# Two gate tiles, wide copies and other homes for batch 0's sums in a fused attention and gated-convolution kernel

## The chip, the cores and the metric

The kernel runs on one core of a Trainium2 chip. The core has five engines, each with its own instruction stream that is worked off in order: TensorE (PE in the profile; its weight loads are PEld), VectorE (DVE), ScalarE (ACT), GpSimd (POOL) and SyncE (SP), which here only issues loads. An engine that reaches an instruction whose inputs are not there stands still, with all that is queued behind it. TensorE writes into PSUM, eight banks of 128 partitions x 512 fp32 values; GpSimd has no part in PSUM here, so whatever TensorE produces is read by VectorE or ScalarE. The metric is the device time of one execution in microseconds (us); lower is better.

## The reference

`x` is [4, 12800, 128] (four batches of 12800 rows), `inducing` is [32, 128]; all outputs are fp32.

```python
def mab(q, kv):                                   # softmax attention
    s = scale * (q @ kv.transpose(0, 2, 1))       # scale = 1/sqrt(128)
    s = s - s.max(-1, keepdims=True)
    a = np.exp(s)
    a /= a.sum(-1, keepdims=True) + 1e-09
    return a @ kv
h = mab(I, x)            # stage 1: 32 queries over all 12800 rows -> h [32, 128] per batch
y = mab(x, h)            # stage 2: each row of x over the 32 rows of h
gate = 1 / (1 + np.exp(-conv(y)))                 # causal depthwise convolution with 5 taps along the rows
out = (gate * (y @ w_val)) @ w_out
```

Stage 2 of a batch cannot begin before its `h` is complete, and `h` needs every row of the batch.

## The kernel before, in words

Each batch is cut into seven units of 2048 rows (one of them 512; "w = 512" and "w = 128" in the code, per group of four). A unit of stage 1 loads `x` transposed (tile `xT`, 1 MB), forms the scores with four matmuls (`a_mm`, tile `s`), takes their maximum and transposes them on VectorE (`a_max`, `a_tr`, tile `e`). When all seven maxima of the batch are there, the batch's maximum `mb` is made (`p_ml` to `p_mc`); then each unit subtracts it (`a_sub`), takes exp on ScalarE (`a_exp`), adds to the sums (`a_z`) and multiplies with `x` in row layout (`a_h`, tile `h`, reading tile `xk`). `p_z`, `p_h` and `p_hq` finish `h`, and `p_v` to `p_we` fold `h`, the taps and `w_val` into small stationary weights `wstk`.

A unit of stage 2 has the scores of its rows (`b_mm`), a softmax over 32 values spread over VectorE, GpSimd and ScalarE (`b_tr` to `b_norm`), the way back to a matmul operand in two fp16 halves (`b_back`, `b_hi`, `b_lo`, tile `hl`), then the gate (`c_gate`, 60 matmuls on four 32-row strips, 4 PSUM banks, tile `g`), two tanh (`c_tanh`), the value product (`c_val`, 12 matmuls, tile `v` in the same four banks, so it starts when both tanh have read the gate), gate times value on VectorE (`c_gv`, two halves, tile `gt`), four output matmuls (`c_out`, tile `o`, two banks in turn) and their copies (`c_ev`, tile `os`), after which the unit is stored.

For batches 1 to 3 the row layout `xk` is loaded (`load_k`). For batch 0 it is made on the chip (`MADE(b)`): TensorE transposes four 128x128 blocks of `xT` into one bank of the four-bank tile `gp` (`a_kt`), and a 512-wide copy carries the bank to `xk` (`a_ke`). The four banks are one tile to the layer that places the waits. Batch 0's made tiles live in `xk` buffers for four units and in `xT` buffers for three (`TAGK`), so that only nine of the twelve `xT` buffers take loads at first.

The order of every engine's instructions is fixed when the program is built. `stage1` and `stage2` add tasks with an engine, a cost in us, a key and dependences; `Plan.order` is a list scheduler that picks the task that can start first, among those within `SLACK` of it the one with the lowest key. `KA` to `KS` and `OUTK` set the keys (`OUTK` says how late the output matmuls come), `BUFS` the number of buffers by tag.

Of the kernel before, what the change touches and what calls it, by code (L numbers as in the profile page):

```python
# [18 lines left out]
P = 128  # L19
M = 32  # L20
# [17 lines left out]
BUFS = dict(xT=12, xk=4, e=7, q=3, m=2, z=2, p=2, hl=3, gt=4, os=2, nm=2, wst=2, wst2=2, gsc=2, hq=2, s=1, x=1, o=2, g=1, gp=4)  # L38
# [3 lines left out]
SLACK = 0.14  # L42
OUTK = 1.21
KA, KB, KH, KC, KP, KS = -4.5, 0.69, 0.0, 0.5, 3.59, 1.94
# [3 lines left out]
def TAGK(b, u):  # L48
    return "xk" if 1 <= u <= BUFS["xk"] else "xT"

# [95 lines left out]
def tile_kernel(ctx: ExitStack, tc: tile.TileContext, xT, xk, inducing, w_val, conv_w, w_out, out):  # L146
# [89 lines left out]
    def load_k(b, u):  # L236
        t0, w = units(b)[u]
        n = w // M
        x = st[b, u, "xk"] = sbt("xk", [P, 16, P])
        nc.sync.dma_start(x[:, :n, :], xk[b, :, t0 // P:t0 // P + n, :])  # L240


    def a_kt(b, u, j):
        w = units(b)[u][1]
        if "gp" not in c_:
            c_["gp"], c_["gpn"] = ps("gp", "g", [P, G, 512]), 0
        k = st[b, u, j, "gp"] = c_["gpn"] % G
        c_["gpn"] += 1
        x = st[b, u, "xT"][:, :G * w].rearrange("p (t i) -> p i t", t=P)
        for i in range(4):  # L250
            T.transpose(c_["gp"][:, k, P * i:P * i + P], x[:, 4 * j + i], c_["identf"])  # L251

    def a_kx(b, u):
        st[b, u, "xk"] = sbt("xk", [P, 16, P], tag=TAGK(b, u))

    def a_ke(b, u, j, eng):
        k = st[b, u, j, "gp"]
        o = st[b, u, "xk"][:, 4 * j:4 * j + 4, :].rearrange("p i c -> p (i c)")
        if eng == "ACT":
            S.copy(o, c_["gp"][:, k, :])  # L260
        else:
            V.tensor_copy(o, c_["gp"][:, k, :])
# [43 lines left out]
    def a_sub(b, u):  # L306
        n = units(b)[u][1] // M
        e = st[b, u, "e"]
        Gp.tensor_tensor(e[:, :n], e[:, :n], bat[b]["mb"].broadcast_to([P, n, M]), ALU.subtract)  # L309
# [7 lines left out]
    def a_z(b, u, v):  # L317
# [3 lines left out]
        if "za" not in d:  # L321
            d["za"] = sbt("za", [P, 16, M])
        if MADE(b):
            V.tensor_reduce(d["za"][:, v, :], e[:, :n].rearrange("p i j -> p j i"), AX.X, ALU.add)  # L324
        elif v == 0:
# [4 lines left out]
    def a_h(b, u, v):  # L330
# [4 lines left out]
        e, x = st[b, u, "e"], st[b, u, "xk"]  # L335
        for i in range(n):
            s = i % G
            T.matmul(d["h"][M * s:M * s + M, :P], e[:, i, :], x[:, i, :],  # L338
# [3 lines left out]
    def p_z(b):  # L342
        d = bat[b]
        zl = d["zl"] = sbt("zl", [P, M])
        n = NU if MADE(b) else 16
        V.tensor_reduce(zl, d["za"][:, :n].rearrange("p i j -> p j i"), AX.X, ALU.add)
# [150 lines left out]
    def strips(b, u, bank, d, k, first, last):  # L497
        w = units(b)[u][1]
        h, wst = st[b, u, "hl"], bat[b]["wst"]
        for i, (part, wp) in enumerate(((0, 0), (0, 1), (1, 0))):  # L500
            for g in range(G):
                s = slice(M * g, M * g + M)
                T.matmul(bank[:, g, :w], wst[s, wp, k, :], h[s, part, 4 - d:4 - d + w],  # L503
                         start=first and i == 0, stop=last and i == 2, tile_position=(M * g, 0))

    def c_gate(b, u):
        bank = st[b, u, "g"] = ps("g", "g", [P, G, 512])
# [3 lines left out]
    def c_tanh(b, u, i):  # L511
        w = units(b)[u][1]
        t = st[b, u, i, "t"] = sbt("gt", [P, 2, 512])
        S.activation(t[:, :, :w], st[b, u, "g"][:, 2 * i:2 * i + 2, :w], AF.Tanh, scale=bat[b]["gsc"])  # L514

    def c_val(b, u):
        bank = st[b, u, "v"] = ps("v", "g", [P, G, 512])
        strips(b, u, bank, 0, TAPS, True, True)

    def c_gv(b, u, i):  # L520
        w = units(b)[u][1]
        t = st[b, u, i, "t"]
        V.scalar_tensor_tensor(t[:, :, :w], t[:, :, :w], 1.0, st[b, u, "v"][:, 2 * i:2 * i + 2, :w], ALU.add, ALU.mult)  # L523
# [37 lines left out]
    def stage1(b):  # L561
# [3 lines left out]
        made = [st[c, u, "kl"][0] for c in range(b) if MADE(c) for u in range(NU)]  # L565
        order = [(v + 1) % NU if b == 0 else v for v in range(NU)]
        kxs = {}
        if MADE(b):
            for u in order:
                kxs[u] = add("NONE", 0.0, -2000, a_kx, (b, u), alloc=TAGK(b, u))  # L570
            made = list(kxs.values())
        for v, u in enumerate(order):
            w = units(b)[u][1]
            key = KEY1(b, v)
            lt = st[b, u, "lt"] = last = add("SP", l(w, 0.1, 2.55), b * NU + v, load_t, (b, u), deps=[last] + made, alloc="xT", lat=2.0)
# [5 lines left out]
            xk, kx = [], kxs.get(u)  # L581
            if MADE(b):
                for j in range(w // P):
                    kt = add("PE", 0.46, -92.9 + 0.01 * v, a_kt, (b, u, j), deps=[lt] + xk[:1], uses=[lt], alloc="gp")
                    eng = "DVE" if v >= NU - 2 and j % 2 else "ACT"
                    xk.append(add(eng, 0.6, -92.9 + 0.01 * v, a_ke, (b, u, j, eng), deps=[kx], uses=[kt, kx]))
                gps.extend(xk)
            st[b, u, "kl"] = [kx] + xk
        if not MADE(b):
            for v, u in enumerate(order):  # L590
                w = units(b)[u][1]
                lk = last = add("SP", l(w, 0.1, 2.55), b * NU + v, load_k, (b, u), deps=[last], alloc="xk", lat=2.0)
                st[b, u, "kl"] = [lk]
# [7 lines left out]
        for v, u in enumerate(order):  # L601
# [3 lines left out]
            su = add("POOL", l(w, 0.3, 1.1), key, a_sub, (b, u), deps=[mc], uses=[tr])  # L605
            ex = add("ACT", l(w, 0.25, 0.64), key, a_exp, (b, u), deps=[su], uses=[tr])
            if MADE(b):
                z = add("DVE", l(w, 0.25, 0.68), key, a_z, (b, u, v), deps=[ex], uses=[tr])
                zs.append(z)
            else:  # L610
                z = add("POOL", l(w, 0.3, 1.1), key + 0.5, a_z, (b, u, v), deps=[ex] + ([z] if z else []), uses=[tr])
                zs = [z]
            lk = st[b, u, "kl"]
            if v == 0:
                h0 = h = add("PE", l(w, 0.25, 1.0), key, a_h, (b, u, v), deps=ph[b - 1:b] + [ex] + lk, uses=[tr] + lk[:1], alloc="x")
            else:
                h = add("PE", l(w, 0.25, 1.0), key, a_h, (b, u, v), deps=[ex, h] + lk, uses=[tr, h0] + lk[:1])
        k = KEYP(b)
        z = add("DVE", 0.35 if MADE(b) else 0.68, k, p_z, (b,), deps=zs)
# [16 lines left out]
    def stage2(b):  # L636
        nonlocal outs
        for u in range(NU):
# [17 lines left out]
            va = add("PE", l(w, 0.19, 0.76), key - 0.3, c_val, (b, u), deps=th, uses=[hi], alloc="g")  # L656
# [61 lines left out]
```

## Time and profile before

| what | value |
|---|---|
| time, median of 3 | 356.49 us (355.5 to 357.47) |
| profiled execution | 354.77 us, of which the span from first to last instruction is 352.9 us |
| PE busy | 313.2 us (89% of the span), mean granted clock 0.968 |
| DVE, ACT, POOL busy | 210.8, 171.1, 156.3 us |
| HBM traffic | 72.4 MB, 205 GB/s over the span |
| chain that ended last | PE 73%, ACT 9%, DVE 8%, POOL 5% of the span |

Times inside a trace are us from the span's start. A row of a timeline or of the chain of waits gives the start, the length, the engine and line, and how many instructions are merged ("x8"); one fp32 matmul of the program is two records, so the four matmuls of `a_mm` read "x8" and one output matmul "x2". A row of a window gives each engine's busy time in a stretch and the clock that TensorE was granted there.

### The profile page before, as it was taken

To read this page: it belongs to the slowest core of one execution; us is meant where nothing else is said; L and a number is where in the kernel's file an instruction comes from. 1 tells how busy PE (TensorE), PEld (TensorE's weight loads), DVE (VectorE), ACT (ScalarE), POOL (GpSimd) and SP (SyncE) were. 2 spreads that over 40 slices of the span, in tenths; PEclk is the share of its full clock that TensorE was granted. 3 is DMA by queue.
4 is the path that set the end of the run, shared out by engine and by line. 5 is a ranking of instruction groups with operands and counts; after the bars stand their busy time and mean duration, and the time that the engine had idled before them with its cause. 6 is when DMAs were issued, how large, how long until landed. Compare 5 with 4: busy or idle time off the path is not lost.

```text
span 352.9 us, 8963 instructions
## 1 busy us (share of the span) xinstructions
PE 313.2 (89%) x3818; PEld 134.2 (38%) x3818; DVE 210.8 (60%) x413; ACT 171.1 (48%) x280; POOL 156.3 (44%) x251
## 2 busy tenths in 40 slices
PE   3786867789989999999999999999999998897773
PEld 1444552233633333345433333444433433332331
DVE  1543397974277977754677785755497776532220
ACT  1343412354554545575455445456745655634453
POOL 0000713753994133489943235599653555421000
PEclk9998795899999999999999999999999999989998
DMA  8970059910998555948966649573222231132223
GB/s 308 418 287 2 0 157 405 413 43 3 347 398 323 182 215 178 391 178 326 394 267 238 241 164 381 235 261 129 121 121 119 121 150 69 53 122 121 119 121 150
DMA packets 11474, 72.95 MB, mean 207 GB/s; under 512 B 1285, under 2 KB 1578, under 8 KB 2986
## 3 DMA queue, kind: packets, MB, share of 16 engines
q1 hardware_dynamic: 7056, 45.88, 33.9%
q10 hardware_dynamic: 4378, 26.50, 18.9%
q8 instruction: 30, 0.49, 0.6%
q14 instruction: 10, 0.08, 0.1%
HBM read 46.16 MB, written 26.21 MB: 205 GB/s over the span
## 4 chain that ended last, share of the span: by engine, by line
PE 73%; ACT 9%; DVE 8%; POOL 5%; issue 2%; DMA 1%; ACTq 0%; DVEq 0%; POOLq 0%
PE o L528 25%; PE g L503 22%; PE s L439 6%; PE s L271 5%; PE gp L251 5%; PE v L503 4%; ACT gt L514 4%; PE h L338 3%; ACT xk L260 3%; DVE gt L523 2%; POOL e L309 2%; DVE za L324 1%; ACT os L535 1%; DMA ind<-in_inducing_dram 1%; PE wt L424 1%
## 5 line engine op out<-in xcount | busy, mean ns | idle before, releaser
L528 PE MATMUL o<-gt,wo 128*128 128x512 f32 (+1 forms) x224 | 105.7, 587 | 8.0 <-DVE gt L523 6.1
L503 PE MATMUL g<-hl,wstk 32*128 32x512 f16 (+1 forms) x1680 | 86.3, 352 | 0.0
L535 ACT COPY os<-o 128x512 f32<-128x512 f32 (+1 forms) x112 | 58.7, 542 | 56.0 <-PE o L528 52.1
L523 DVE SCALAR_TENSOR_TENSOR gt<-gt,v 128x1024 f32<-128x1024 f32 (+1 forms) x56 | 59.5, 1098 | 36.8 <-ACT os L535 27.8
L503 PEld LDWEIGHTS <-wstk 32*128 32x128 f16 x2016 | 45.0, 93 | 79.1 <-issue 20.0
L514 ACT ACTIVATE gt<-g,gsc 128x1024 f32<-128x1024 f32 (+1 forms) x56 | 54.3, 1017 | 31.6 <-PE g L503 31.5
L528 PEld LDWEIGHTS o<-gt,wo 128*128 128x128 f32 x224 | 36.0, 191 | 53.3 <-issue 34.2
L309 POOL TENSOR_TENSOR e<-e,mb 128x512 f32<-128x512 f32 (+1 forms) x28 | 32.0, 1160 | 42.9 <-DVE mb L304 42.7
L471 POOL TENSOR_TENSOR q<-q,z 128x512 f32<-128x512 f32 (+1 forms) x28 | 26.8, 956 | 48.5 <-DVE z L466 23.8
L487 POOL TENSOR_TENSOR hl<-p,hl 128x512 f16<-128x512 f32 (+1 forms) x28 | 29.5, 1054 | 34.7 <-ACT hl L482 34.4
L454 POOL TENSOR_TENSOR q<-q,m 128x512 f32<-128x512 f32 (+1 forms) x28 | 26.7, 955 | 32.4 <-DVE m L449 31.4
L271 PE MATMUL s<-xT,iw 128*32 128x512 f32 (+1 forms) x224 | 28.7, 589 | 3.6 <-issue 2.1
L439 PE MATMUL s<-xT,hq 128*32 128x512 f32 (+1 forms) x224 | 30.1, 612 | 1.7 <-DVE hq L367 1.1
L444 DVE STREAM_TRANSPOSE q<-s 128x512 f32<-128x512 f32 (+1 forms) x28 | 18.1, 645 | 21.4 <-PE s L439 21.3
L464 DVE TENSOR_REDUCE z<-q 128x16 f32<-128x512 f32 (+1 forms) x28 | 17.3, 618 | 20.0 <-ACT q L459 19.9
L482 ACT CAST hl<-p 128x512 f16<-128x512 f32 (+1 forms) x28 | 16.0, 574 | 25.3 <-DVE p L476 24.0
L275 DVE TENSOR_REDUCE nm<-s 128x1 f32<-128x512 f32 (+1 forms) x28 | 17.5, 625 | 16.3 <-PE s L271 16.2
L459 ACT ACTIVATE q<-q 128x512 f32<-128x512 f32 (+1 forms) x28 | 16.4, 585 | 21.9 <-POOL q L454 21.5
L338 PE MATMUL h<-xk,e 128*32 128x128 f32 x800 | 25.8, 274 | 0.0
L260 ACT COPY xk<-gp 128x512 f32<-128x512 f32 x23 | 13.0, 587 | 25.9 <-PE gp L251 25.9
L251 PE MATMUL gp<-identf,xT 128*128 128x128 f32 x100 | 17.9, 317 | 8.4 <-ACT xk L260 7.6
L338 PEld LDWEIGHTS h<-xk,e 128*32 128x32 f32 x800 | 21.1, 110 | 10.9 <-issue 6.9
(86 smaller groups left out, 242.9 us busy)
## 6 DMA issues: line engine op xcount, KB each, us to landing
xT<-in_xt_dram SPq DMA_DIRECT2D x24, 1024.0 KB, 8.7
out_dram<-os ACTq DMA_DIRECT2D x24, 1024.0 KB, 4.4
xk<-in_xk_dram SPq DMA_DIRECT2D x18, 1024.0 KB, 8.9
xT<-in_xt_dram SPq DMA_DIRECT2D x4, 256.0 KB, 5.0
out_dram<-os ACTq DMA_DIRECT2D x4, 256.0 KB, 2.5
xk<-in_xk_dram SPq DMA_DIRECT2D x3, 256.0 KB, 6.4
raw<-in_moe_w_val_dram ACTq DMA_DIRECT2D x1, 128.0 KB, 7.4
raw<-in_moe_w_out_dram ACTq DMA_DIRECT2D x1, 128.0 KB, 9.9
```

What stands on the lines that cost most here:

```text
L251: T.transpose(c_["gp"][:, k, P * i:P * i + P], x[:, 4 * j + i], c_["identf"])
L271: T.matmul(sc[M * g:M * g + M, :w], c_["iw"], x[:, w * g:w * g + w], start=True, stop=True, tile_position=(0, M * g))
L309: Gp.tensor_tensor(e[:, :n], e[:, :n], bat[b]["mb"].broadcast_to([P, n, M]), ALU.subtract)
L338: T.matmul(d["h"][M * s:M * s + M, :P], e[:, i, :], x[:, i, :], start=v == 0 and i < G, stop=v == NU - 1 and i >= n - G, tile_position=(0, ...
L439: T.matmul(sc[M * g:M * g + M, :w], bat[b]["hq"], x[:, w * g:w * g + w], start=True, stop=True, tile_position=(0, M * g))
L471: Gp.tensor_tensor(q[:, :n], q[:, :n], st[b, u, "z"][:, :n].broadcast_to([P, n, M]), ALU.mult)
L487: Gp.tensor_tensor(h[:, 1, 4:4 + w], st[b, u, "p"][:, :w], h[:, 0, 4:4 + w], ALU.subtract)
L503: T.matmul(bank[:, g, :w], wst[s, wp, k, :], h[s, part, 4 - d:4 - d + w], start=first and i == 0, stop=last and i == 2, tile_position=(M * ...
L514: S.activation(t[:, :, :w], st[b, u, "g"][:, 2 * i:2 * i + 2, :w], AF.Tanh, scale=bat[b]["gsc"])
L523: V.scalar_tensor_tensor(t[:, :, :w], t[:, :, :w], 1.0, st[b, u, "v"][:, 2 * i:2 * i + 2, :w], ALU.add, ALU.mult)
L528: T.matmul(op[:, :w], bat[b]["wo"], st[b, u, g // 2, "t"][:, g % 2, :w], start=True, stop=True)
L535: S.copy(os[:, w * g:w * g + w], st[b, u, g, "o"][:, :w])
```

## The change

1. The four gate banks become two tiles of two banks, `g0` and `g1`. Batch 0's transposes now fill eight blocks (two banks) at a time, in turns between the two tiles, and one 1024-wide ScalarE copy takes each away; VectorE makes no such copies any more.
2. `c_val` writes over the gate's own tiles instead of a newly allocated one. For batch 3 alone (`PAIRS`) it is issued in two halves of six matmuls, each on two strips and one tile, and each waits for its own tanh; `c_gv` of a half waits for that half.
3. For batch 0 the maximum is subtracted on VectorE instead of GpSimd, and the sums are made by TensorE (four matmuls of a block of ones with `e`, accumulated in a bank, tile `zp`) instead of seven VectorE reductions; `p_z` folds that bank and divides by 32.
4. Batch 0's made tiles live in one `q`, four `xk` and four `gt` buffers (`HOME`), so all twelve `xT` buffers take loads, and the loads no longer wait for the made tiles.
5. The planner's constants and the costs of a few tasks are other numbers; `OUTK` goes from 1.21 to 1.6.

```diff
-BUFS = dict(xT=12, xk=4, e=7, q=3, ... s=1, x=1, o=2, g=1, gp=4)
+BUFS = dict(xT=12, xk=4, e=7, q=3, ... s=1, x=1, o=2, g=1, g0=1, g1=1, gp=2)
-SLACK = 0.14
-OUTK = 1.21
-KA, KB, KH, KC, KP, KS = -4.5, 0.69, 0.0, 0.5, 3.59, 1.94
+SLACK = 0.17
+OUTK = 1.6
+KA, KB, KH, KC, KP, KS = -4.5, 0.68, 0.89, 0.52, 3.76, 1.83
+def HOME(u):
+    return [("q", 4)] if u == 0 else [("xk", 16)] if u <= 4 else [("gt", 8), ("gt", 8)]
+def PAIRS(b):
+    return b == 3
 def a_kt(b, u, j):
-    k = st[b, u, j, "gp"] = c_["gpn"] % G
+    n = min(8, w // M)
+    k = c_["gpn"] = 1 - c_.get("gpn", 1)
+    t = st[b, u, j, "gp"] = ps("gp", f"g{k}", [P, 2, 512])
-    for i in range(4):
-        T.transpose(c_["gp"][:, k, P * i:P * i + P], x[:, 4 * j + i], c_["identf"])
+    for i in range(n):
+        T.transpose(t[:, i // 4, P * (i % 4):P * (i % 4) + P], x[:, 8 * j + i], c_["identf"])
 def a_ke(b, u, j, eng):
-        S.copy(o, c_["gp"][:, k, :])
+        S.copy(o, i)                      # i: both banks, 128 * n wide
 def a_sub(b, u):
-        Gp.tensor_tensor(e[:, :n], e[:, :n], bat[b]["mb"].broadcast_to([P, n, M]), ALU.subtract)
+        (V if MADE(b) else Gp).tensor_tensor(e[:, :n], e[:, :n], bat[b]["mb"].broadcast_to([P, n, M]), ALU.subtract)
 def a_z(b, u, v):
-        if MADE(b):
-            V.tensor_reduce(d["za"][:, v, :], e[:, :n].rearrange("p i j -> p j i"), AX.X, ALU.add)
+        if MADE(b):
+            if v == 0:
+                d["zp"] = ps("zp", "s", [P, P])
+            for s in range(G):
+                T.matmul(d["zp"][M * s:M * s + M, :k * M], c_["ones"][:, :M], e[:, k * s:k * s + k, :].rearrange("p i j -> p (i j)"),
+                         start=v == 0, stop=v == NU - 1, tile_position=(0, M * s))
+            return
 def p_z(b):
-        V.tensor_reduce(zl, d["za"][:, :n].rearrange("p i j -> p j i"), AX.X, ALU.add)
+        z = d["zp"].rearrange("p (i j) -> p j i", j=M) if MADE(b) else d["za"].rearrange("p i j -> p j i")
+        V.tensor_reduce(zl, z, AX.X, ALU.add)
+        if MADE(b):
+            V.tensor_scalar(zl, zl, 1.0 / M, None, ALU.mult)
 def c_gate(b, u):
-        bank = st[b, u, "g"] = ps("g", "g", [P, G, 512])
+        bank = st[b, u, "g"] = [ps("g", f"g{i}", [P, 2, 512]) for i in range(2)]
-def c_val(b, u):
-        bank = st[b, u, "v"] = ps("v", "g", [P, G, 512])
-        strips(b, u, bank, 0, TAPS, True, True)
+def c_val(b, u, i):
+        bank = st[b, u, "g"]
+        strips(b, u, bank, 0, TAPS, True, True, range(2 * i, 2 * i + 2) if PAIRS(b) else range(G))
 ...
-                lt = ... add("SP", ..., load_t, (b, u), deps=[last] + made, alloc="xT", lat=2.0)
+                lt = ... add("SP", ..., load_t, (b, u), deps=[last], alloc="xT", lat=2.0)
-            su = add("POOL", l(w, 0.3, 1.1), key, a_sub, (b, u), deps=[mc], uses=[tr])
+            su = add("DVE" if MADE(b) else "POOL", ..., key, a_sub, (b, u), deps=[mc], uses=[tr])
+            if PAIRS(b):
+                va = [add("PE", l(w, 0.2, 0.7), key - 0.3, c_val, (b, u, i), deps=[th[i]], uses=[hi, ga]) for i in range(2)]
```

What this does to the order of the instructions shows at three places.

TensorE at the start of the program, before (`s` is a score tile, `gp` the transposed blocks; the bracket names the semaphores that a row waits for):

```order
L271 MATMUL s_103<-xT,iw 32x512 [waits DMAHW0_49,DVE_49]
L271 MATMUL s_103<-xT,iw 32x512 x3
L251 MATMUL gp<-identf,xT 128x128 x4
L251 MATMUL gp<-identf,xT 128x128 [waits Activation_49]
L251 MATMUL gp<-identf,xT 128x128 x3
L271 MATMUL s_123<-xT,iw 32x512 [waits DMAHW2_49]
```

and now:

```order
L280 MATMUL s_105<-xT,iw 32x512 [waits DMAHW0_49,DVE_49]
L280 MATMUL s_105<-xT,iw 32x512 x3
L256 MATMUL gp<-identf,xT 128x128 x16
L280 MATMUL s_134<-xT,iw 32x512 [waits DMAHW2_49]
L280 MATMUL s_134<-xT,iw 32x512 x3
L256 MATMUL gp<-identf,xT 128x128 [waits Activation_49]
L256 MATMUL gp<-identf,xT 128x128 x7
```

Before, the second group of four transposes waits for a copy; now the first wait for a copy stands ahead of the third group of eight, behind the next unit's score matmuls.

TensorE and VectorE where batch 0's sums are made. VectorE before (`za` the partial sums, `zl` their fold, `nm` and the transposition into `e` belong to batch 1):

```order
L324 TENSOR_REDUCE za_356<-e_202 128x32 [waits Activation_49]
L275 TENSOR_REDUCE nm_309<-s1_358 128x1 [waits PE_49]
L324 TENSOR_REDUCE za_356<-e_233 128x32 [waits Activation_49]
L324 TENSOR_REDUCE za_356<-e_254 128x32 [waits Activation_49]
L324 TENSOR_REDUCE za_356<-e_281 128x32 [waits Activation_49]
L346 TENSOR_REDUCE zl_463<-za_356 128x32 [waits DVE_49]
L280 STREAM_TRANSPOSE e_465<-s1_358 128x512 [waits PE_49]
L351 COPY hs_471<-h_336 128x128 [waits PE_49]
```

and now:

```order
L318 TENSOR_TENSOR e_254<-e_254,mb_337 128x512
L318 TENSOR_TENSOR e_281<-e_281,mb_337 128x512
L318 TENSOR_TENSOR e_299<-e_299,mb_337 128x128
L284 TENSOR_REDUCE nm_330<-s1_331 128x1 [waits PE_49]
L289 STREAM_TRANSPOSE e_423<-s1_331 128x512 [waits PE_49,Activation_49]
L284 TENSOR_REDUCE nm_330<-s1_340 128x1
L289 STREAM_TRANSPOSE e_446<-s1_340 128x512 [waits PE_49,Activation_49]
L368 COPY hs_496<-h_349 128x128 [waits PE_49]
L361 TENSOR_REDUCE zl_498<-zp_370 128x32 [waits PE_49]
L363 TENSOR_SCALAR zl_498<-zl_498 128x32 [waits DVE_49]
```

The seven reductions are gone from VectorE, the seven subtractions stand there instead, and the fold of the sums waits for TensorE.

TensorE in the last batch, one full unit, before (`gt_4377` and `gt_4382` are the halves of this unit's `gt`, `gt_4253` is the second half of the unit ahead of it; the eleven other rows of `v` are left out, and likewise below):

```order
L528 MATMUL o_4375<-gt_4253,wo_3724 128x512 [waits Activation_49]
L528 MATMUL o_4380<-gt_4253,wo_3724 128x512 [waits Activation_49]
L503 MATMUL v_4388<-hl_4135,wstk_3758 128x512 [waits Activation_49]
...
L528 MATMUL o_4413<-gt_4377,wo_3724 128x512 [waits DVE_49,Activation_49]
L528 MATMUL o_4415<-gt_4377,wo_3724 128x512 [waits Activation_49]
```

and now, the same place (`gt_4384` and `gt_4390` are this unit's, `gt_4270` and `gt_4279` those of the unit ahead of it):

```order
L546 MATMUL o_4382<-gt_4270,wo_3820 128x512 [waits Activation_49]
L546 MATMUL o_4388<-gt_4279,wo_3820 128x512 [waits Activation_49]
L520 MATMUL g_4309<-hl_4172,wstk_3850 128x512 [waits Activation_49]
...
L520 MATMUL g_4310<-hl_4172,wstk_3850 128x512 [waits Activation_49]
...
L546 MATMUL o_4407<-gt_4279,wo_3820 128x512 [waits Activation_49]
L456 MATMUL s2_4412<-xT_2813,hq_3697 32x128 x4
L546 MATMUL o_4424<-gt_4384,wo_3820 128x512 [waits DVE_49,Activation_49]
```

Before, both output matmuls behind the value product need this unit's `gt`; now the first of them takes the last quarter of the unit ahead, and only the second needs this unit's first half.

89 lines of the change are left out of this document (47 added, 42 removed).

## The prediction

> **What bounds the kernel now.** I read the stretches first, then the start and the end of the chain of waits, then the groups by form for prices. The windows:
>
> ```profile
> 0.00:80.00 80.00, 56.83 (x663) 30.55 (x667) 46.73 (x106) 28.53 (x53) 22.38 (x41) 0.89 0.57 224
> 80.00:170.00 90.00, 88.76 (x1174) 36.86 (x1166) 58.13 (x106) 48.10 (x72) 53.52 (x73) 1.00 0.68 260
> 170.00:265.00 95.00, 94.10 (x1189) 37.81 (x1177) 65.62 (x138) 50.77 (x83) 54.72 (x89) 1.00 0.60 226
> 265.00:353.00 88.00, 73.48 (x809) 28.96 (x808) 40.33 (x64) 43.69 (x73) 25.69 (x49) 0.97 0.28 115
> ```
>
> The columns are the busy times of PE, PEld, DVE, ACT and POOL, then the clock granted to TensorE, the DMA share and GB/s. From 80 to 265 us TensorE is idle for 1.24 + 0.90 = 2.1 us: there it is the bound. It is idle for 23.2 us before 80 and for 14.5 us after 265, and these are the two places that the change touches. What is saved at the start moves the full middle forward whole; what is saved at the end comes straight off.
>
> At the start the chain goes to and fro between transposes (gp) and copies (xk); then comes the row that ends it:
>
> ```profile
> 8.07 1.06 PE gp L251 x4
> ...
> 10.51 0.99 PE s L271 x8
> 11.50 1.11 PE gp L251 x8
> ...
> 27.52 0.59 ACT xk L260
> ...
> 28.16 0.73 PE gp L251 x4
> ...
> 28.92 0.59 ACT xk L260
> ...
> 29.55 0.73 PE gp L251 x4
> ...
> 37.21 1.86 PE s L271 x8
> ```
> ```profile
> 37.25 0.19 DVE L304 COPY mb<-t 128x32 f32<-128x32 f32 x1 [1.88 <-PE t L299]
> 37.52 7.89 POOL L309 TENSOR_TENSOR e<-e,mb 128x512 f32<-128x512 f32 x7 [36.20 <-DVE mb L304]
> 43.86 4.77 PE L338 MATMUL h<-xk,e 128*32 128x128 f32 x168
> 51.48 0.38 PE L356 MATMUL t<-zl,ones 128*128 128x32 f32 x2 [2.85 <-DVE zl L346]
> ```
>
> Four blocks cost 29.55 − 28.16 = 1.39 us, of which TensorE works half. The maximum `mb` is there at 37.4, the last product with `x` ends at 48.6, and TensorE waits until 51.48 for VectorE's fold of the sums. Loads do not explain this: they stop early.
>
> ```profile
> GB/s 308 418 287 2 0 157 405 413 43 3 347 398 323 182 215 178 391 178 326 394 267 238 241 164 381 235 261 129 121 121 119 121 150 69 53 122 121 119 121 150
> ```
>
> A slice is 8.82 us: 6.4 MB have come by 17.6 us and 8.9 MB by 26.5. Batch 0's seven loads and the weights are 6.8 MB, so (estimate from these slices) they are in by about 19 us.
>
> At the end the chain repeats one pattern; `v` is the value product, "gt L514" the tanh, "gt L523" gate times value:
>
> ```profile
> 281.44 3.38 PE g L503 x60
> ...
> 294.64 1.91 PE o L528 x4
> 296.55 1.00 PE s L439 x8
> 297.55 0.79 PE v L503 x12
> ...
> 323.14 3.38 PE g L503 x60
> 326.53 0.02 issue
> 326.55 2.12 ACT gt L514 x2
> 328.67 0.97 ACT os L535 x2
> 329.64 0.03 issue
> 329.67 1.23 DVE gt L523
> 330.90 0.14 issue
> 331.03 1.96 PE o L528 x4
> 332.99 3.38 PE g L503 x60
> ...
> 342.83 0.95 PE g L503 x60
> ```
>
> A full unit takes 332.99 − 323.14 = 9.85 us. TensorE's own work in it is a gate 3.38, a value product 0.79 and four outputs at 0.95, 8.0 us in all. It is idle while the second tanh ends and while VectorE makes the first half of `gt`. The copies named at 328.67 were not what VectorE waited for: the value product ran beside them and ended last.
>
> **The start, term by term.** Prices:
>
> ```profile
> L260 ACT COPY xk<-gp 128x512 f32<-128x512 f32 x23 | 13.0, 587 | 25.9 <-PE gp L251 25.9
> L514 ACT ACTIVATE gt<-g,gsc 128x1024 f32<-128x1024 f32 x48 | 51.0, 1108 | 28.8 <-PE g L503 28.7
> L324 DVE TENSOR_REDUCE za<-e 128x32 f32<-128x512 f32 x6 | 6.0, 1054 | 0.0
> L216 DVE TENSOR_TENSOR w<-w 128x384 f32<-128x384 f32 x1 | 0.5, 516 | 0.0
> L314 ACT ACTIVATE e<-e 128x512 f32<-128x512 f32 x24 | 14.8, 630 | 13.4 <-POOL e L309 12.7 <-POOL za L326 0.4
> ```
>
> A 1024-wide PSUM copy has no row. Its bounds are the tanh's 1.11 and two narrow copies, 1.17. TensorE needs 1.11 for eight blocks and a further 0.5 for its share of a unit's scores, 1.6 per copy. With two tiles in turns the copy is hidden at either bound. So TensorE sets the pace: 100 transposes at 1.11 per eight (13.9), five more full score groups at 1.0 and the small one at 0.25, about 0.5 for the slow first matmuls, all from 8.07, where the first scores have just ended: 27.7 us. No load is late for that, since the last unit's scores are due at about 23. The two small matmuls and the two small reductions of the maximum take about 1.1 more, and `mb` is there at 28.9 instead of 37.44: **8.5 us**.
>
> The subtraction on VectorE has no row either. L216 (two fp32 operands) bounds it from below at 0.52, the strided L324 from above at 1.05; it is nearest to L216, and scaled to 512 that is 0.69. Only the first lies on the path, against 1.28 on GpSimd: 0.6 us. VectorE's queue holds two score groups of batch 1 behind the subtractions; nobody needs these before `p_h`. TensorE meanwhile has those two groups' score matmuls (2.0 us), so the products with `x` start at about 30.5, after the first exp (0.63). They are 200 records, 4.77 / 168 = 0.0284 each: 5.7 us.
>
> The sums add 7 x 4 matmuls, 56 records of the form of L338 (32 stationary columns, 128 moving, the same four positions): 1.6 us. Were each as slow as a transpose (1.11 / 8 = 0.139 a record), it would be 7.8; I take L338, whose form it is. One product with its sums is 1.1 us, above 0.69, so TensorE and not VectorE sets the pace. It ends at 37.8. Fold, rescale and copy on VectorE are 128x32 and 128x128 forms, together under 1 us with two handovers, so `p_h` comes at 38.8 instead of 51.48: 12.7. I take **12.3** for what I cannot see. Up to the first full gate the same chain follows as now, so the shift passes on. GpSimd is only relieved. The five early loads of batch 1 queue behind batch 0's and the next waits for batch 0's second-stage scores, as now.
>
> The clock is the unsure part (columns as in the first windows):
>
> ```profile
> 28.16:33.72 5.56, 3.01 (x17) 2.23 (x17) 1.02 (x6) 2.34 (x4) 0.00 (x0) 0.96 0.00 0
> 33.72:39.10 5.38, 4.91 (x20) 2.36 (x21) 0.47 (x2) 1.93 (x4) 1.58 (x2) 0.50 0.00 0
> 54.20:63.60 9.40, 7.82 (x78) 2.44 (x74) 7.58 (x27) 2.82 (x7) 3.93 (x9) 0.50 1.01 415
> ```
>
> At half clock a score group takes 1.86 (the row at 37.21) instead of 0.99. The stretch from 33.72 follows 7 us in which TensorE did nothing but spaced transposes. In the new order there are 36 transposes between the last scores of batch 0 and the scores of batch 1, about 4.5 us, dense. I reckon with full clock.
>
> The Trainium skill ("TensorE: Matmul & The Clock Gate", section "Part 4: PE-mode transpose") says that transposes do not count as TensorE activity for its clock gate in the way matmuls do. The row at 33.72 agrees, though spacing explains it as well; by that rule the second rival below would be the likelier case.
>
> **The middle.** `c_val` in the gate's own tile waits for the same two tanh as the fresh tile did. Each gate now waits for VectorE's second half of `gt`, 2.35 + 0.26 us after the value product. In the new order TensorE has at least two outputs and half a product with `x` in between (2.4 us), mostly 2.9: **+0.3** in all.
>
> **The end.** A half of the value product has three steps of two strips where the whole has three of four: 0.40 if strips cost alone, 0.79 if steps do. Steps do in the gate (60 matmuls in 3.38 us are 15 steps of 0.22), so I take 0.66, that is 0.5 us more per unit. For a full unit after its gate: two outputs (1.9) cover the first tanh; first half 0.66; second half 0.66, from 2.56, its tanh ending at 2.25; the leftover output of the unit ahead (0.95) while VectorE makes the first half of `gt` (2.56 + 1.23 and two handovers: ready at 4.05); the unit's first output from 4.17. The next gate starts at 5.1, as the second half of `gt` ends: 8.5 us instead of 9.85, TensorE full.
>
> From the batch's first gate to its last, small one it is 342.83 − 281.44 = 61.4 us now. Filled, it is six gates 20.3, six value products 7.9, 21 large outputs and two small ones (a quarter each) 20.5, and 2.25 of scores: 51.0. One score group and a small output, 1.2 us, move ahead of that stretch into time that is full already. This leaves 9.2; I take **8.5** for waits behind ScalarE's and VectorE's queues. Bounds: 0 if these queues keep the old pace, 9.2.
>
> **Sum.** 354.77 (profiled execution, 352.9 span and 1.9 around it) − 12.3 + 0.3 − 8.5 = 334.3. The median of the runs shown is 356.49, 1.7 above the profiled one: **336**.
>
> **Rivals.** (1) *Half clock through the products*: two score groups lose 1.9, the first products and their sums some 1.5: 336 + 3.4 = 339.4. For it the row at 33.72, against it that TensorE is dense there. (2) *Copies still alternate with transposes*: per eight blocks 1.11 + 1.1 + 0.1 = 2.3 instead of 2.78, 28.9 us from 8.07 on; the products end at about 45.5 and `p_h` comes at 46.5, 5 us earlier instead of 12.3: 343.3. Against it one wait per eight blocks in the order, with 16 before the first. (3) *The end does not fill*: the softmax chain for the next unit (VectorE, GpSimd and ScalarE in turn) or ScalarE's copies hold the outputs back, and the dearer value product eats the rest: 344.5. For it the outputs' wait for copies, against it that these engines are half idle from 265 on. (4) *Slower*: the gate's wait for the second half of `gt` is not covered in the middle. It decides from 20.5 / 18.75 = 1.1 us per full unit of batches 0 to 2; wholly uncovered it is 2.6, 336 + 49 = 385. Against it the 2.4 to 2.9 us counted above. The change not doing what it says is (2).
>
> **How the numbers follow.** Forecast 0.60 (332 to 338.5), (1) 0.18, (2) 0.05, (3) 0.13, (4) 0.04. The range reaches down to 331 (9.2 at the end, 12.7 at the start, and some of the slow clock from 54.2 gone) and up to 345, which takes in (1) to (3). A measurement of this kernel cannot tell less than 0.5%, 1.8 us, from no change. All cases but (4) lie 11 us or more below: faster 0.96; of (4) 0.01 falls within 0.5% and 0.03 above.
>
> **What would show it.** Right: transposes in rows of x16 and wide copies of 1.1; `mb` near 29, `p_h` near 39, the first full gate near 57 instead of 69; the last batch's gates 8.5 apart. Wrong: granted clock 0.5 between 27 and 36 (1); the gate's rows waiting for "DVE gt" in the middle (4); gates still over 9.5 apart at the end (3). I would be most wrong if TensorE turned out not to be full between 70 and 250.

## The result, and the profile after

The changed kernel takes **338.72 us** (median) against 356.98 us for the kernel before on the same chip; the ratio is **0.948**, 95% interval 0.943 to 0.954. The forecast was 336. One of its four executions took 1038.64 us, for a reason that no kept trace shows, and the ratio goes by the other three, which took 338.25 to 338.89. The profiled execution took 338.89 us, of which the span is 337.1 us.

The windows of the changed kernel, with the columns explained above:

```profile
57.00:70.00 13.00, 12.41 (x153) 4.93 (x145) 7.30 (x14) 5.24 (x10) 4.69 (x11) 1.00 0.06 22
70.00:165.00 95.00, 89.25 (x1099) 36.28 (x1100) 60.73 (x108) 50.31 (x74) 56.69 (x76) 0.98 0.67 260
...
252.00:327.00 75.00, 74.73 (x827) 28.65 (x826) 44.43 (x82) 42.50 (x68) 25.63 (x49) 1.00 0.26 106
```

The end is now full: from 252 to 327 us TensorE idles for 0.3 us. The middle, which was full before, is not: from 70 to 165 us TensorE idles for 95.00 − 89.25 = 5.75 us.

The start of the chain of waits (start, length, engine and tile, records):

```profile
8.48 3.61 PE gp L256 x16
12.09 1.33 PE s L280 x8
13.42 2.00 PE gp L256 x16
...
29.03 1.85 PE s L280 x16
30.88 0.90 PE h L353 x32
31.78 0.22 PE zp L335 x8
...
38.60 0.38 PE t L373 x2
```

Transposes run sixteen at a time with no wait for a copy; a product with `x` and its sums take 0.87 to 0.90 + 0.22 us, six times, and a quarter of that for the small unit; `p_h` (L373) comes at 38.60 instead of 51.48. The prices that had no row before now have one (groups by form, VectorE and ScalarE):

```profile
L318 DVE TENSOR_TENSOR e<-e,mb 128x512 f32<-128x512 f32 x6 | 3.7, 687 | 0.0
```
```profile
L269 ACT COPY xk<-gp 128x1024 f32<-128x1024 f32 x12 | 11.8, 1015 | 15.2 <-PE gp L256 15.2
```

The end of the chain:

```profile
309.02 3.36 PE g L520 x60
312.38 1.91 PE o L546 x4
314.29 1.11 PE g L520 x12
315.40 1.05 PE o L546 x2
316.45 0.07 issue
316.53 1.10 PE o L546 x2
317.62 3.36 PE g L520 x60
...
326.23 0.96 PE g L520 x60
```

A unit takes 317.62 − 309.02 = 8.60 us instead of 9.85, and in it the chain leaves TensorE for 0.07 us only. `x12` are the two halves of the value product, 1.11 us together.

The hole in the middle, in TensorE's timeline:

```profile
85.27 1.98 PE L546 MATMUL o<-gt,wo 128*128 128x512 f32 x4
90.82 1.56 PE L280 MATMUL s<-xT,iw 128*32 128x512 f32 x8 [3.57 <-DMA xT<-in_xt_dram]
92.08 2.01 PE L353 MATMUL h<-xk,e 128*32 128x128 f32 x32
94.02 1.43 PE L546 MATMUL o<-gt,wo 128*128 128x512 f32 x2
95.38 1.07 PE L280 MATMUL s<-xT,iw 128*32 128x512 f32 x8
...
164.63 1.07 PE L280 MATMUL s<-xT,iw 128*32 128x512 f32 x8 [2.19 <-DMA xT<-in_xt_dram]
```

and in SP's (one row is a run of loads, from the first issue to the last):

```profile
43.93 38.11 SPq L246 DMA_DIRECT2D xk<-in_xk_dram  x7
82.09 2.35 SPq L239 DMA_DIRECT2D xT<-in_xt_dram  x5
```

TensorE stands for 3.57 us before the first scores of batch 2 and for 2.19 us before those of batch 3. After the first wait a group of scores, a product and an output take 4.56 us (90.82 to 95.38) where they take 2.9 at full rate (85.89 to 88.81 in the first experiment): half rate for a while, 1.6 us more. The load that TensorE waits for was issued at 82.09, behind seven `xk` loads of which the last three wait until products of batch 1 free their buffers, and landed 8.6 us later. In the 13 us from 57 to 70 the DMA engines had been 6% busy.

Split at the first full gate and at the first full gate of batch 3, in us of the span:

| stretch | before | after | difference | forecast |
|---|---|---|---|---|
| to the first full gate | 69.17 | 55.89 | −13.3 | −12.3 |
| from there to batch 3's first full gate | 212.3 | 218.6 | **+6.4** | +1.5 (0.3 and the 1.2 moved ahead) |
| from there to the end of the span | 71.5 | 62.6 | −8.9 | −9.7 |
| span | 352.9 | 337.1 | −15.8 | −20.5 |

### The profile page after: what moved, and what is told of

It reads as the page before. It is cut to its first block, busy times and chain, and to the rows that moved or that the text cites. A ratio compares the mean times of both kernels' runs of the same rounds, so it can differ in the third digit from the quotient of the medians.

```text
span 337.1 us, 9075 instructions
## 1 busy us (share of the span) xinstructions
PE 313.0 (93%) x3874; PEld 136.3 (40%) x3874; DVE 207.6 (62%) x412; ACT 171.2 (51%) x270; POOL 148.4 (44%) x244
## 4 chain that ended last, share of the span: by engine, by line
PE 85%; DMA 6%; DVE 3%; ACT 2%; POOL 1%; issue 1%; SPq 0%; ACTq 0%; POOLq 0%
PE g L520 30%; PE o L546 27%; PE s L280 7%; PE s L456 7%; PE h L353 7%; DMA xT<-in_xt_dram 5%; PE gp L256 4%; DMA ind<-in_inducing_dram 1%; PE wt L441 1%; POOL hl L504 1%; ACT gt L531 1%; ACT os L553 0%; DVE z L481 0%; PE zp L335 0%; PE t L308 0%
## 5 line engine op out<-in xcount | busy, mean ns | idle before, releaser
L520 PE MATMUL g<-hl,wstk 32*128 32x512 f16 (+1 forms) x2016 | 110.3, 352 | 0.5 <-ACT gt L531 0.5
L541 DVE SCALAR_TENSOR_TENSOR gt<-gt,g 128x1024 f32<-128x1024 f32 (+1 forms) x56 | 59.5, 1098 | 44.2 <-PE g L520 44.0
L520 PEld LDWEIGHTS <-wstk 32*128 32x128 f16 x2016 | 45.9, 92 | 75.6 <-issue 35.3
L353 PE MATMUL h<-xk,e 128*32 128x128 f32 x800 | 28.2, 281 | 0.0
L318 POOL TENSOR_TENSOR e<-e,mb 128x512 f32<-128x512 f32 (+1 forms) x21 | 24.1, 1156 | 7.7 <-DVE mb L313 6.8
L499 ACT CAST hl<-p 128x512 f16<-128x512 f32 (+1 forms) x28 | 16.1, 575 | 22.3 <-DVE p L493 20.5
L353 PEld LDWEIGHTS h<-xk,e 128*32 128x32 f32 x800 | 21.9, 112 | 12.6 <-issue 5.7
L493 DVE STREAM_TRANSPOSE p<-q 128x512 f32<-128x512 f32 (+1 forms) x28 | 17.9, 641 | 8.0 <-POOL q L488 7.8
L342 POOL TENSOR_TENSOR za<-za,e 128x512 f32<-128x512 f32 (+1 forms) x18 | 20.5, 1141 | 2.1 <-ACT e L323 1.7
```

The source lines that it names most:

```text
L318: (V if MADE(b) else Gp).tensor_tensor(e[:, :n], e[:, :n], bat[b]["mb"].broadcast_to([P, n, M]), ALU.subtract)
L353: T.matmul(d["h"][M * s:M * s + M, :P], e[:, i, :], x[i], start=v == 0 and i < G, stop=v == NU - 1 and i >= n - G, tile_position=(0, M * s))
L520: T.matmul(bank[g // 2][:, g % 2, :w], wst[s, wp, k, :], h[s, part, 4 - d:4 - d + w], start=first and i == 0, stop=last and i == 2, tile_p ...
```

## The experiments

All times are medians and are compared with the changed kernel's 338.72, which was not measured again beside them. The kernel before was: its medians there are 356.9 to 359.4 us, so differences of 1 to 2 us between kernels are near the limit of what these runs can tell.

### The middle: the loads ahead

```diff
 seq = plan.order()
+for b in range(1, B - 1):        # in the finished order, only SP's loads are moved
+    at = ... load_k(b, 4)
+    for u in range(2):
+        ... put load_t(b + 1, u) right ahead of at
```

> Edit: of the loads of batch 2 and of batch 3 the first two xT loads are issued ahead of the last three xk loads of the batch before; nothing else moves on any engine. Theory A (the two waits of TensorE at the first scores of batches 2 and 3, 3.57 and 2.19 us, come from SP's queue: the xT loads stand behind xk loads that wait for products h, while their own buffers are free at about 71.2 and 74.3): both waits go, and the half-rate score group behind the first (1.56 instead of 1.07) with them, about 6 us in all: 332.5 (331 to 334), the first score of batch 2 at about 87.2 and no row 'PE s <- DMA xT'. Theory B (the loads are late because the transfers share the bandwidth, so what is moved ahead holds up the xk loads behind it): the wait turns into 'PE h <- DMA xk' and the time stays within 1.5 us of 338.7.

**330.47 us**, ratio 0.922 (0.917 to 0.926): 8.3 us below the changed kernel, the fastest of all. A window, and a row each of TensorE's and SP's timelines:

```profile
70.00:165.00 95.00, 95.00 (x1216) 38.37 (x1216) 66.59 (x117) 53.35 (x80) 62.06 (x84) 1.00 0.71 275
```
```profile
85.89 1.07 PE L280 MATMUL s<-xT,iw 128*32 128x512 f32 x8
```
```profile
46.37 2.86 SPq L239 DMA_DIRECT2D xT<-in_xt_dram  x2
```

Theory A holds. The order of the other four engines is that of the changed kernel to the last instruction; TensorE doesn't idle at all from 70 to 165 us, the row of batch 2's first scores (85.89) has no wait, and no `xk` load became late. The waits (5.8) and the half-rate rows behind the first (1.6) are 7.4 us; in the two traces the stretch from the first full gate to batch 3's is shorter by 7.6 (211.0 instead of 218.6). The remaining 0.9 of the 8.3 I can't place for certain: this execution's first full gate came 1.3 us earlier (54.59), 0.4 of it with its first input and 0.6 in the first transposes and the scores behind them, on which the loads of batches 2 and 3 have no bearing. The buffers were free even sooner than I had said: the two loads were issued at 46.4 and 48.9, not at 71 and 74.

The same move in the kernel before:

> Edit: the kernel before, with the same move as in loads_ahead (two xT loads of batches 2 and 3 ahead of the last three xk loads of the batch before), and nothing else. Theory A (the kernel before paid little for SP's order: TensorE came to the scores of batch 2 6.2 us after the load was issued and waited 1.24 us, and about 0.9 us in batch 3): 1 to 3 us faster, 354 to 356. So the changed kernel lost about 5 of its gain to this wait, and with the loads ahead in both the change is worth 23 to 25 us. Theory B (the kernel before hid a wait of the same size elsewhere, in another engine's row): 5 us faster or more, and the change itself costs nothing in the middle.

355.53 us, ratio 0.994 (0.991 to 0.997): 2.1 us below the 357.64 beside it, so theory A. In the kernel before the row was

```profile
102.76 1.06 PE L271 MATMUL s<-xT,iw 128*32 128x512 f32 x8 [1.24 <-DVE p L476]
```

which names VectorE; with the loads ahead the idle is gone (timeline of this run):

```profile
104.15 1.04 PE L271 MATMUL s<-xT,iw 128*32 128x512 f32 x8
```

so it had been the load there too, which had been issued at 95.32 and landed 7.3 us later. This wait is 1.24 of the 2.1 us; the 0.81 us for which the kernel before stands near the first scores of batch 3 (ahead of 178.57, for a tanh) is not the load's and stays. The two profiled executions don't differ in the same way, 353.7 us of span against 352.9: the first full gate came 2.6 us later in this one (71.77), and from there on it was 1.8 us shorter. With the loads ahead in both kernels the change is worth 355.53 − 330.47 = 25.1 us; as it was made, 18.3. About 7 us of its gain went into a wait that the kernel before paid only a little for.

### The middle: which numbers made the wait longer

```diff
-SLACK = 0.17
-KA, KB, KH, KC, KP, KS = -4.5, 0.68, 0.89, 0.52, 3.76, 1.83
+SLACK = 0.14
+KA, KB, KH, KC, KP, KS = -4.5, 0.69, 0.0, 0.5, 3.59, 1.94
```

> Edit: SLACK and the six key constants have the numbers of before; OUTK and everything else stay. Theory A (with the new constants TensorE comes to the first score group of batches 2 and 3 before its load has landed, because fewer products h and outputs stand ahead of it, and the load is issued no earlier): the two waits of 3.57 and 2.19 us shrink to 1 to 2 us each and the time falls to 334 to 336 unless the end is filled worse. Theory B (the waits come from the loads alone, from SP's queue and the shared transfers, wherever the order puts the scores): the waits stay between 5 and 6 us in sum and the time within 1.5 us of 338.7.

340.26 us, but its runs lie in two pairs, 337.75 and 338.31, and 342.21 and 343.2; the trace is of the 338.31. Theory A falls with either pair, and theory B's time is that of the lower one. TensorE's timeline has the waits still, 6.3 us of them:

```profile
88.99 1.94 PE L280 MATMUL s<-xT,iw 128*32 128x512 f32 x8 [3.15 <-DMA xT<-in_xt_dram]
...
162.58 1.06 PE L280 MATMUL s<-xT,iw 128*32 128x512 f32 x8 [3.16 <-DMA xT<-in_xt_dram]
```

With `OUTK = 1.21` besides, so that all the planner's free numbers are the old ones:

> Edit: as old_constants, and OUTK at 1.21 as well, so that all of the planner's free numbers are those of the kernel before; tiles, halves, batch 0's start and the buffers stay those of the change. Theory A (the later outputs took away the work that covered the load in the kernel before): the waits for xT in batches 2 and 3 sum to 2.5 us or less and the time is 334 to 337. Theory B (the waits come with the other buffers and start of batch 0, whatever the numbers): 5 to 6.5 us of waits as before, 338 to 341.

```profile
89.28 1.06 PE L280 MATMUL s<-xT,iw 128*32 128x512 f32 x8 [2.12 <-DMA xT<-in_xt_dram]
...
161.90 1.06 PE L280 MATMUL s<-xT,iw 128*32 128x512 f32 x8 [2.40 <-DMA xT<-in_xt_dram]
```

339.56 us, and 4.5 us of waits: the time is theory B's, the waits lie between the theories. Of the numbers only `OUTK` took some of the waits away (6.3 to 4.5); most of them stay. What else was changed (the start, the buffers of batch 0, the tiles, the costs of some tasks) was not taken apart, so where the rest comes from stays open. In batch 2 the rows say only where the 2.3 us between 1.24 and 3.57 lie: TensorE was ready 5.2 us after the load's issue (82.09 to 87.25) instead of 6.2 (95.32 to 101.52), and its scores started 8.7 us after it (90.82) instead of 7.4 (102.76).

The planner thinks that a load lands 2 us after its slot on SP. Told 5 for batches 2 and 3:

```diff
-lt = ... load_t, (b, u), deps=[last], alloc="xT", lat=2.0)
+lt = ... load_t, (b, u), deps=[last], alloc="xT", lat=5.0 if b > 1 else 2.0)
```

> Edit: for batches 2 and 3 the planner is told that an xT load lands 5 us after its slot on SP instead of 2; loads keep their order on SP. TensorE's first score group of batches 2 and 3 now stands behind the next unit's gate, about 5.3 us of work later (a product h 0.9, an output 1.06, a gate 3.35). Theory A (a planner that takes a load to land sooner than it does put TensorE's scores where their data cannot be): the score group of batch 2 is reached at about 92.6, after the load has landed at 90.7; both waits go as with the loads ahead, and the time is 331 to 334. Theory B (batch 2's scores are on the way to its h, so what TensorE gains there it pays later, when the first gates of batches 2 and 3 come late): 336 to 339.

336.43 us, ratio 0.942 (0.934 to 0.950). The waits for `xT` are gone, and the scores of batch 2 start at 92.50 as expected, but only 2.3 us are won, theory B's number. The window shows what is left:

```profile
70.00:165.00 95.00, 91.62 (x1180) 36.95 (x1183) 66.04 (x113) 50.80 (x76) 60.16 (x82) 1.00 0.71 272
```

3.4 us of idle, now in waits for VectorE and ScalarE (its longest: 1.5 us for a score bank that VectorE reads late, 1.0 us for `gt`). Here, moving the work behind the load was not as good as moving the load.

### The start: turns, width, and where the sums are made

One tile of two banks instead of two in turns:

```diff
-t = st[b, u, j, "gp"] = ps("gp", f"g{k}", [P, 2, 512])
+t = st[b, u, j, "gp"] = ps("gp", "g0", [P, 2, 512])
```

> Edit: the transposes of batch 0 use the first of the two tiles alone, eight blocks at a time, with the same wide copies; the order on every engine stays. Theory A (two tiles in turns are what hides the copies): each eight blocks now cost transposes 1.11 plus copy 1.01 plus handover 0.1 less what score groups fill, so that of 12 full copies about 0.6 us each comes back: mb and the first gate about 6 to 8 us later, 345 to 347. Theory B (fewer and wider copies are the gain, the turns are not needed because score groups stand between): within 2 us of 338.7.

350.54 us, ratio 0.979 (0.973 to 0.984): 11.8 us lost, more than either theory said. TensorE's timeline, and the window that begins at 34:

```profile
32.74 1.17 PE L256 MATMUL gp<-identf,xT 128*128 128x128 f32 x8 [1.10 <-ACT xk L269]
...
35.01 1.97 PE L256 MATMUL gp<-identf,xT 128*128 128x128 f32 x8 [0.95 <-ACT xk L269]
...
39.70 2.79 PE L280 MATMUL s<-xT,iw 128*32 128x512 f32 x16
```
```profile
34.00:42.00 8.00, 6.16 (x32) 3.60 (x35) 2.83 (x9) 3.79 (x6) 0.00 (x0) 0.57 0.00 0
```

TensorE waits for copies for 7.3 us in seven rows of up to 1.10. What theory A missed is that the gaps also cost the clock: from 34 to 42 us it is 0.57, eight transposes take 1.97 instead of 1.17 and two groups of scores 2.79 instead of 1.92.

Two copies of one bank each instead of one of two:

```diff
-S.copy(o, i)
+for c in range(0, P * n, 512):
+    S.copy(o[:, c:c + 512], i[:, c:c + 512])
```

> Edit: each wide copy of two banks becomes two copies of one bank, 512 wide; the two tiles in turns stay. Theory A (the copies are hidden behind the other tile's transposes and a share of scores, 1.6 us per eight blocks against 2 x 0.59): no change, 338.7 within 1 us. Theory B (ScalarE's time per block counts): per eight blocks 1.17 instead of 1.01, 12 copies, at most 2 us more, and mb later by as much.

338.65 us: theory A. The copies have 13.0 us (25 of 0.596) instead of 12.4, all hidden. The turns matter; that the copies are wide doesn't show.

Sums of batch 0 on VectorE again (`a_z` and `p_z` of the kernel before):

> Edit: batch 0's sums are made by seven reductions on VectorE again, 1.05 us each, folded as before; the subtractions of the maximum stay on VectorE, so both now stand in its queue. Theory A (the sums on VectorE were the last thing that p_h waited for): TensorE saves 1.6 us of sums, but VectorE needs 0.56 + 1.05 per unit besides two score groups of batch 1, so p_h comes about 4 to 5 us later and the time is 343 (341 to 345). Theory B (the sums hide beside the products and the gain at the start is the copies' alone): 337 to 339.

341.33 us, 2.6 more: theory A's mechanism, about half its price.

```profile
33.92 2.83 PE L350 MATMUL h<-xk,e 128*32 128x128 f32 x96 [1.89 <-ACT e L323]
37.89 0.43 PE L350 MATMUL h<-xk,e 128*32 128x128 f32 x8 [1.14 <-ACT e L323]
39.91 0.38 PE L368 MATMUL t<-zl,ones 128*128 128x32 f32 x2 [1.59 <-DVE e L289]
```

VectorE alternates subtractions and sums, so ScalarE's exp and then the products starve (1.89 and 1.14), and the fold comes last. From batch 1's first scores to `p_h` it is 27.46 to 39.91, 12.45 us, instead of 9.64 (28.96 to 38.60).

The subtraction on GpSimd again, sums on TensorE:

> Edit: batch 0's maximum is subtracted on GpSimd again (7.89 us for seven, 1.12 each); the sums stay on TensorE and TensorE's order is the same. Theory A (with products and sums at 1.09 us a unit the pace of GpSimd is about the same, so only the first subtraction and the gaps count): p_h 0.6 to 1.5 us later, 339.3 to 340.2. Theory B (the subtraction on VectorE is worth more, as each unit now waits for GpSimd, ScalarE's exp and a handover): 341 or more.

340.77 us (its runs 340.18 to 342.3), 2.0 more. The same stretch takes 11.02 us, 1.4 more, inside theory A; the first exp makes TensorE wait 0.46 us and the later units follow at GpSimd's pace: their products start 1.24 us apart, where 1.09 is TensorE's own, and one subtraction takes 1.286 us (its group by form, six of 512).

The time itself lies between the theories. The remaining 0.6 of the 2.0 is not explained; it is less than one slow stretch of the clock costs (1.7 us, last section), and the two traces don't have them at the same places.

### The start: transposes and the clock

```diff
-for i in range(n):
+for i in [i for i in range(n) for _ in range(3 if u in (0, 6) else 1)]:
     T.transpose(t[:, i // 4, ...
```

> Edit: each of the last 20 transposes of batch 0 (units 6 and 0) is issued three times in a row, to the same place; 40 more transposes, 0.139 us each, 5.6 us, so that TensorE does nothing but transposes for about 10 us instead of 4.3 ahead of batch 1's scores. Theory A (what lowers the granted clock is that TensorE stands idle between spaced transposes; dense ones hold it): 338.7 + 5.6 = 344.3 (343 to 346), the two score groups after them at 1.92 for sixteen records. Theory B (transposes do not count as activity for the clock gate, as the Trainium skill says in 'TensorE: Matmul & The Clock Gate', section 'Part 4: PE-mode transpose', and 4.3 us were only too short to show it): the later transposes run at half rate, 1.97 per eight, the two score groups take 3.6 to 3.9 and the first products are slow: 349 to 353.

343.02 us, 4.3 more: theory A. TensorE's timeline, and the window over the transposes:

```profile
23.66 3.89 PE L256 MATMUL gp<-identf,xT 128*128 128x128 f32 x32
...
27.63 2.96 PE L256 MATMUL gp<-identf,xT 128*128 128x128 f32 x24
...
32.41 1.92 PE L280 MATMUL s<-xT,iw 128*32 128x512 f32 x16
```
```profile
23.60:32.40 8.80, 8.80 (x79) 8.43 (x72) 2.83 (x9) 3.25 (x4) 0.00 (x0) 1.00 0.88 367
```

For 8.8 us TensorE does nothing but dense transposes, apart from three tiny matmuls, and the granted clock stays 1.00; the scores behind them take 1.92 as ever. Together with the single tile this tells idle gaps from transposes: dense transposes hold the clock, and spaced ones with nothing else between them lost it. Where groups of scores stood between the transposes, the single tile's 1.10 us gaps left the clock at 1.00 too (14 to 34 us).

### The end: halves

`PAIRS` returns False, so batch 3's value products are whole:

> Edit: batch 3's value products are one piece again, as for the other batches; the two tiles, OUTK and the constants stay, and the planner orders the end anew. Theory A (the halves are what fills the end: gate times value of the first half starts before the second tanh's half is done): the last units return to a gate 3.38, then two tanh 2.2, value product 0.79, 1.23 on VectorE and two outputs 1.96, 9.6 to 9.85 us instead of 8.6, over six periods 6 to 7.5 us: 345 to 346. Theory B (the later outputs, OUTK 1.6, and the gate's own tile filled it; the halves only cost 0.3 us a unit): 336.5 to 339.

343.26 us, 4.5 more: theory A's mechanism, at two thirds of its price. TensorE's timeline:

```profile
293.19 3.42 PE L520 MATMUL g<-hl,wstk 32*128 32x512 f16 x60
296.54 1.98 PE L546 MATMUL o<-gt,wo 128*128 128x512 f32 x4
...
300.91 1.96 PE L546 MATMUL o<-gt,wo 128*128 128x512 f32 x4 [1.27 <-ACT hl L499]
302.80 3.42 PE L520 MATMUL g<-hl,wstk 32*128 32x512 f16 x60
```

The unit takes 9.6 us, and the 1.27 is the first half of gate times value, as in the kernel before; later units name "DVE gt". From the first gate to the last it is 331.64 − 273.65 = 58.0 us, against 51.7 with halves: 6.3 of the 9.7 us won there are the halves', and whole products give 1.4 back at the tail. The other 3.4 go to the new order and are not split further.

Halves in all four batches, on top of the loads ahead:

> Edit: loads_ahead with the value products of all four batches in halves; the planner orders the program anew. Theory A (halves cost TensorE 1.11 instead of 0.79 a unit, and where it is full they fill nothing): 18 full units by 0.32 = 5.8 us more than 330.5: 336 (334 to 338). Theory B (a half that waits for its own tanh leaves the order more room, and TensorE had waits of this kind in the middle): 331 or less.

340.30 us, 9.8 more than with halves in batch 3 alone: theory A's direction, a higher price. The planner orders the program anew, so not all of this is the halves'. In the traces the stretch from the first full gate to batch 3's takes 220.2 us instead of 211.0, of which 1.7 are a first gate at a lower clock (5.11 instead of 3.42), and the last batch, which is in halves in both, takes 2.0 more. That leaves 7.5 us for 18 full units, 0.42 a unit where 0.32 was expected. TensorE's timeline shows where the halves are dear:

```profile
108.51 0.82 PE L520 MATMUL g<-hl,wstk 32*128 32x512 f16 x6
...
110.46 0.82 PE L520 MATMUL g<-hl,wstk 32*128 32x512 f16 x6
```

Where other work stands between the halves each takes about 0.75 (0.82 less the overlap with the row behind), as much as a whole product. Back to back they take about 1.1 together.

## Why the prediction was right or wrong

**The total.** 338.72 measured, 336 forecast: inside the range of 331 to 345, and 0.2 us above the likeliest case's own (332 to 338.5). Part of that agreement is luck. In spans the forecast was −20.5 and the measurement −15.8, 4.7 short. But I had carried over that the profiled execution of before lay 1.7 us under its median; that of after lies 0.2 above, which gave back 1.9.

**The start, right.** `mb` was there at 29.26 (28.9 forecast), the last product ended at 37.7 (37.8), `p_h` came at 38.60 (38.8), the first full gate at 55.89 ("near 57"). The bounded prices: subtraction 0.687 (0.69), wide copy 1.015 (below its bounds of 1.11 and 1.17), product and sums 1.09 (1.1), all sums 1.5 (1.6). Two errors cancelled: the first sixteen transposes and the scores behind them cost 1.9 us over the later ones, not 0.5, and dense transposes take 1.00 per eight, not 1.11. The start was mis-sized by 1.0 at the first full gate: 0.4 that I kept back for what I could not see, 0.2 at `p_h`, and 0.4 on the way from `p_h` to the gate (17.29 us instead of 17.69).

**Rival 1 (half clock), fell.** The granted clock held, behind 28 transposes (29.03: 1.85 for sixteen records of scores) as behind 68. The Trainium skill's statement that transposes do not count as TensorE activity ("TensorE: Matmul & The Clock Gate", "Part 4: PE-mode transpose"), by which this rival would have been likelier (the prediction calls it the second; it is the first), isn't borne out here: 8.8 us of transposes kept 1.00. The row at 33.72 of the kernel before fits spacing, by which the single tile lost the clock too.

**Rival 2 (copies still alternate), fell**, and it was underpriced: the kernel that does alternate takes 350.5 us, not 343.3.

**The middle, wrong: this is the step that failed.** "+0.3 in all" counted one new wait, that of a gate for the second half of `gt`. That wait never appeared (one row "PE g <- ACT gt" of 0.5 us is all). The stretch grew by 6.4 instead of 1.5, from a wait that I had not looked for: the first scores of batches 2 and 3 wait for their loads, 5.8 us, and the half rate after the first costs 1.6. The kernel before had stood for 2.1 us there, 1.24 for the load of batch 2 and 0.81 for a tanh; with the 1.2 us of work moved in from the end, 7.4 − 2.1 + 1.2 = 6.5 is about what was measured. I had dismissed loads with the start ("Loads do not explain this: they stop early") and followed SP's queue only through batch 1. The loads ahead show the cause and the price: without this wait the change is worth 25 us. I had named the symptom, a TensorE that is not full between 70 and 250 us, as what would make me most wrong, but the only case that I had for it was rival 4, with another mechanism.

**The end, right.** 8.9 from batch 3's first gate on, with forecast 8.5 for the end after the 1.2 moved ahead, 9.7 without: first gate to last 51.7 (51.0 if filled), units 8.6 apart (8.5), "fills" rather than rival 3. The halves cost 1.11 together where I had 1.32; that saved 0.2 a unit and paid for the small waits. The sequence was the one worked out: counted from the end of a gate, the unit's first output starts at 316.53 − 312.38 = 4.15 (4.17) and the next gate at 5.24 (5.1).

## What to carry to other kernels

When a change moves the start of a pipeline, follow every in-order queue through the whole program, the loads' queue first: ask for each load what stands ahead of it, what that waits for, and whether its own buffer has long been free. A wait of 1.2 us in a full stretch is a warning that its cover is nearly used up, and here moving the load cost nothing, while moving the work behind it put other waits in its place. Take turns between two PSUM tiles before widening copies, and split work in two only where the engine has holes to fill.

## What the runs showed of the hardware that I had not expected

- **Gaps and the clock.** Nine kernels wait twice for `xT`. Of the nine waits of 3.1 to 3.6 us six were followed by a stretch at half clock, and so were three of the nine of 2.1 to 2.6 us, here with the narrow copies (at full rate these rows of the product and the gate read 1.08 and 3.42):

```profile
163.28 1.07 PE L281 MATMUL s<-xT,iw 128*32 128x512 f32 x8 [2.23 <-DMA xT<-in_xt_dram]
164.14 1.85 PE L354 MATMUL h<-xk,e 128*32 128x128 f32 x32
165.92 4.28 PE L521 MATMUL g<-hl,wstk 32*128 32x512 f16 x60
```

  The gap of 2.1 to 2.3 us ahead of the first full gate, which all fourteen kernels have, was followed by such a stretch in seven kernels. Each of these stretches lasts 3.4 us by the trace's clock entries, so it costs 1.7, and two executions can differ by one or more of them. The Trainium skill ("TensorE: Matmul & The Clock Gate", "Why this matters for your kernels") puts the limit at gaps of about 3 us; these runs show no such limit, as shorter gaps lost the clock and longer ones kept it. In the single-tile run repeated gaps of only 1.1 us between transposes also ended at half rate, while the 8.8 us of dense transposes did not.
- **A slow beginning.** The first sixteen transposes took 3.61 us against 2.0 later, and they differ between runs (timeline rows of 2.76 to 3.68); the first full gate moves with them by about a microsecond. The clock's column shows 1.00 there, but the trace has no entry for the clock yet: its first one, full clock, comes at 12.7 us of the span, in the middle of the scores that took 1.33. In ten other kernels with two tiles it comes at 9.6 to 11.7 us, and with the single tile at 14.2, behind transposes that took 1.97 per eight. So the first rows ran at a lower clock; what sets the moment is open.
- **Queued loads.** Where TensorE waited, the window showed the DMA engines full:

```profile
87.25:95.40 8.15, 4.58 (x47) 2.52 (x46) 2.31 (x5) 1.21 (x2) 4.23 (x6) 0.79 1.01 420
```

  The 1 MB load issued there, with others in the queue, landed 8.6 us later. The two that were moved ahead took 14.5 us, longer, and nothing waited for them, as they had been issued 39 us before their scores; what mattered was the issue time, not the transfer.
